# Which queue issues the output stores: double tiles from POOL, half tiles from SyncE

## The chip, the cores and the metric

The kernel runs on one core of a Trainium2 chip. The metric is device time in microseconds (us) of that core, from six runs. The profile is of one execution of its own.

The engines are named as in the profile: PE (TensorE, matmuls) and PEld (its weight loads), DVE (VectorE), ACT (ScalarE), POOL (GpSimd), SP (SyncE). A DMA is issued by an engine into a queue and carried out by 16 DMA engines. In this program the DMAs that POOL issues run on the queue q0, which the profile calls software_dynamic, and those that SyncE issues on q1, hardware_dynamic.

## The reference

The input `x` has 8 sequences of 3264 rows of 192 channels, float32. Two steps follow each other:

```python
# 1: causal convolution over 7 rows, one set of softmax taps per head (8 heads of 24 channels)
w = softmax(weight, axis=-1)
a[b, s] = sum over k of w[h, k] * x_padded[b, s + k]
# 2: spectral mix of the first 64 modes, then a channel mix
X = np.fft.rfft(a, axis=1)
Yr = einsum(Xr, w_r) - einsum(Xi, w_i)      # per mode, 192 x 192
Yi = einsum(Xr, w_i) + einsum(Xi, w_r)
y = np.fft.irfft(Y, n=S, axis=1)
u = a + y
out = u + np.maximum(u @ w_ch, 0.0)
```

The output has the shape of `x`, in float32: 8 x 3264 x 192 x 4 bytes = 20.05 MB.

## The kernel before

The eight sequences are worked on as four pairs, `q` from 0 to 3. A sequence's 3264 rows are 25 tiles of 128 rows (`t` from 0 to 24) and a rest of 64 rows, the half tile. `xall` holds all of the sequences in bfloat16, `slot(q, t)` being the place of one tile of both sequences of a pair.

The kernel has three stages. In the first, `x` is loaded by POOL's DMAs (line 149, cast from float32 to bfloat16 on the way), convolved on PE, copied back into `xall` and transformed into the 64 modes. In the second, the mode weights are loaded, again by POOL (line 426), into buffers in `arena` and in a part of `cc`, and mixed. Both queues and the order on each engine are as written in the program: the schedule is manual.

The third stage, from about 107 us on, makes the output. It goes through the list `duos` (line 530). An item is

- two tiles that follow each other in one pair, `((q, t), (q, t + 1))`: the first four pairs, each with two stores of 192 KB (line 578);
- a double tile, the same `t` in two pairs, `((q, t), (q + 1, t))`: 45 of them, each with one store of 384 KB, 512 rows of 768 bytes (line 573);
- one tile of one pair: the last two items, each with a store of 192 KB (line 563);
- `("h",)`, the half tiles of all pairs, item 14, with four stores of 96 KB from 64 partitions each (line 554);
- an integer 1, 2 or 3 (items 2, 8 and 11), which stores nothing: it makes the spectral coefficients `zw` of that pair.

That makes N = 55 items. For each, PE adds up in a PSUM tile `zt` (four of them, `za` and `zb`, in turn): `c_part` (lines 487 and 494), then `m_part` with which = 0 (line 514), then ACT's `relu` in place (line 540), then `m_part` with which = 1. `finish` (from line 542) has DVE add `xall` to it into a buffer of `outs` (lines 546, 560 and 565), and then the store is issued. The loop at line 622 puts `m_part(n, 0)`, `c_part(n + 1)`, `m_part(n - 1, 1)` and `finish(n - 1)` after one another, so that PE works on three items by turns.

`outs` is six buffers of 3,072 bytes per partition, cut out of `arena`, which holds the mode weights before. Item n uses `outs[n % NO]` with NO = 6. DVE's add into a buffer waits until the store that read the buffer before has landed. An engine issues its DMAs in the order of the program: a store that waits for its add holds back what stands behind it on that engine.

`band` (line 78) holds the taps of the convolution as matrices, 2,048 bfloat16 per partition; nothing reads it after the first stage.

Of the kernel before, what the change touches and what calls it, by code (L numbers as in the profile page):

```python
# [12 lines left out]
F32 = mybir.dt.float32  # L13
# [6 lines left out]
def kernel(  # L20
# [9 lines left out]
    nc = tc.nc  # L30
# [22 lines left out]
    def sb(name, shape, dtype, **kw):  # L53
        return pool.tile([P] + shape, dtype, tag=name, name=name, **kw)
# [23 lines left out]
    band = sb("band", [H, 2 * P], BF16)  # L78
# [18 lines left out]
    NO = 6  # L97
    OB = 2 * 2 * 2 * D
    outs = [arena[:, OB * i:OB * (i + 1)].bitcast(F32).rearrange("p (k d) -> p k d", k=2) for i in range(NO)]
    assert NO * OB <= NW * WGB  # L100
    pos = [0]

    def temp(n, dtype):
# [36 lines left out]
    def slot(q, t):  # L140
        return NT * q + t
# [48 lines left out]
    for g in range(4):  # L190
        dst, srcv = band[32 * g:32 * g + 32, :, 32 * g:32 * g + PW], pk3[32 * g:32 * g + 32, :, :]
# [213 lines left out]
    for k, u in enumerate(units):  # L405
# [5 lines left out]
        if k:  # L411
            q, t0, n = units[k - 1]
# [117 lines left out]
    duos = [((q, t), (q, t + 1)) for q in range(2) for t in (0, 2)]  # L530
# [3 lines left out]
    for k, item in ((2, 1), (8, 2), (11, 3), (14, ("h",))):  # L534
        duos.insert(k, item)

    def relu(n):
        duo, zt = items[n]
        w = D * len(duo) if duo[0] != "h" else 2 * D
        nc.scalar.activation(out=zt[:, :, 0:w], in_=zt[:, :, 0:w], func=ACT.Relu)  # L540

    def finish(n):
        duo, zt = items[n]
        o = outs[n % NO]
        if duo[0] == "h":
            nc.vector.tensor_tensor(out=o[:, :, :].rearrange("p k (a d) -> p k a d", a=2),  # L546
                                    in0=zt[:, :, 0:2 * D].rearrange("p k (a d) -> p k a d", a=2),
                                    in1=xall[:, NF:NF + NT * (NQ - 1) + 1:NT, 0, :].rearrange(
                                        "p (k a) d -> p k a d", k=2), op=ALU.add)
            for k in range(2):  # L550
                for h, r in enumerate(ROWS):
                    dst = bass.AP(tensor=out.tensor, offset=out.offset + ((4 * k + (h ^ k)) * S + P * NF) * D,
                                  ap=[[D, HALF], [2 * S * D, 2], [1, D]])
                    nc.gpsimd.dma_start(out=dst, in_=o[r, k, :].rearrange("p (a d) -> p a d", a=2))  # L554
            return
        (q0, t0), (q1, t1) = duo[0], duo[-1]
        s = [slot(*u) for u in duo]
        ov = o[:, :, :].rearrange("p k (i d) -> p (k i) d", i=2)
        if len(duo) == 1:
            nc.vector.tensor_tensor(out=ov[:, 0:2, :], in0=zt[:, :, 0:D], in1=xall[:, s[0], :, :], op=ALU.add)  # L560
            dst = bass.AP(tensor=out.tensor, offset=out.offset + (2 * q0 * S + P * t0) * D,
                          ap=[[D, P], [S * D, 2], [1, D]])
            nc.sync.dma_start(out=dst, in_=ov[:, 0:2, :])
            return
        nc.vector.tensor_tensor(out=o[:, :, :].rearrange("p k (i d) -> p i k d", i=2),  # L565
                                in0=zt[:, :, 0:2 * D].rearrange("p i (k d) -> p i k d", k=2),
                                in1=xall[:, s[0]:s[1] + 1:s[1] - s[0], :, :].rearrange("p k i d -> p i k d"),
                                op=ALU.add)
        if t0 == t1:

            dst = bass.AP(tensor=out.tensor, offset=out.offset + (2 * q0 * S + P * t0) * D,
                          ap=[[D, P], [S * D, 4], [1, D]])
            nc.sync.dma_start(out=dst, in_=ov)
        else:
            for i in range(2):
                dst = bass.AP(tensor=out.tensor, offset=out.offset + ((2 * q0 + i) * S + P * t0) * D,
                              ap=[[D, P], [P * D, 2], [1, D]])
                nc.sync.dma_start(out=dst, in_=ov[:, i:4:2, :])

    N = len(duos)  # L580
# [41 lines left out]
    for n in range(N + 1):  # L622
        if is_duo(n):
            m_part(n, 0)
            relu(n)
        if n + 1 < N and n > 0:
            if is_duo(n + 1):
                c_part(n + 1)
            else:
                q, zt = items[n + 1]  # L630
                for c in range(2):
                    zw_part(q, c, zt[:, c, :])
                for act, w in enumerate(QUARTERS):
                    zw_copy(zw[:, q, :, w, :], zt[:, :, 0:2 * D].rearrange("p c (b e) -> p c b e", b=4)[:, :, w, :],
                            act)
        if is_duo(n - 1):
            m_part(n - 1, 1)
            finish(n - 1)
# [30 lines left out]
```

## Time and profile before

| | |
|---|---|
| median of six runs | 180.71 us (179.86 to 181.94) |
| the profiled execution: time | 180.41 us |
| the profiled execution: span of the profile | 178.6 us |
| PE, DVE, ACT, POOL busy, share of the span | 83%, 66%, 57%, 38% |
| queue q0 (POOL): packets, bytes | 36224, 20.08 MB |
| queue q1 (SyncE): packets, bytes | 26624, 19.69 MB |
| stores of 384 KB (SyncE, line 573): number, median from issue to landing | 45, 4.4 us |
| stores of 192 KB (SyncE, lines 563 and 578) | 10, 2.8 us |
| stores of 96 KB (POOL, line 554) | 4, 3.4 us |
| HBM read, written | 39.40 MB, 20.05 MB |

The bytes of a queue are counted as they arrive: of a load that casts from float32 to bfloat16, half of what was read. "Busy" of an engine leaves out waiting; issuing a DMA counts as busy for POOL, and for SyncE nothing does. "Landing" is the moment at which the last of the 16 DMA engines has reported. In the views of stretches, a line has the stretch, its length, busy time and number of instructions of each engine, TensorE's granted clock (1.00 is full speed), the mean share of the 16 DMA engines' time that packets took, and GB/s.

### The profile page before, as it was taken

Reading aid. Unit: us, or ns where it says so; the run is one execution under the profiler, and the core shown is the slowest. Engines: PE = TensorE matmul, PEld = TensorE weight load, DVE = VectorE, ACT = ScalarE, POOL = GpSimd, SP = SyncE. Lnnn points to the kernel's source line nnn. Section 1 sums busy time; section 2 is a strip of 40 time slices with the busy share of each in tenths; the row PEclk is TensorE's granted clock in tenths of the full one; section 3 lists DMA queues with packets and bytes.
Section 4 is the critical chain, followed back from the end, with each engine's and each line's share of the span. In section 5 each row is a group of like instructions: output and inputs, shape, how many; then the busy total and the mean of one; then the engine's idle time right before and its main releaser. Section 6 shows DMA issues by size and latency. Waiting matters only on the chain.

```text
span 178.6 us, 6302 instructions
## 1 busy us (share of the span) xinstructions
PE 147.4 (83%) x2736; PEld 108.7 (61%) x2736; DVE 117.0 (66%) x161; ACT 101.6 (57%) x135; POOL 68.3 (38%) x113
## 2 busy tenths in 40 slices
PE   0047789999999998794977768999999999999940
PEld 0033466666666665663865656966677888888820
DVE  1879564766866584564456472795787888888870
ACT  8175755544554636174464566766566766666630
POOL 7999997768865643442336100000140000000000
PEclk9999999999999999999699999999999999999995
DMA  4999999999999999999999970569779999999995
GB/s 46 161 177 187 190 190 190 192 192 194 188 191 192 204 206 206 206 206 207 206 206 206 206 117 4 168 230 317 258 210 359 365 346 369 334 364 359 298 370 178
DMA packets 62875, 40.17 MB, mean 225 GB/s; under 512 B 28800, under 2 KB 62784, under 8 KB 62848
## 3 DMA queue, kind: packets, MB, share of 16 engines
q0 software_dynamic: 36224, 20.08, 80.9%
q1 hardware_dynamic: 26624, 19.69, 32.8%
q8 instruction: 21, 0.34, 0.9%
q14 instruction: 6, 0.05, 0.1%
HBM read 39.40 MB, written 20.05 MB: 333 GB/s over the span
## 4 chain that ended last, share of the span: by engine, by line
DMA 41%; PE 35%; POOL 14%; issue 4%; DVE 2%; POOLq 0%; DVEq 0%
DMA xall<-in_x_dram 17%; DMA arena<-in_moe_w_i_dram 12%; POOL xall L149 10%; PE za L514 9%; PE zb L514 8%; PE za L494 8%; DMA cc<-in_moe_w_i_dram 7%; PE zb L494 7%; DMA arena<-in_moe_w_r_dram 6%; DVE arena L565 1%; POOL xall L219 1%; POOL arena L426 1%; PE zb L521 1%; DVE arena L560 1%; PE low L437 1%
## 5 line engine op out<-in xcount | busy, mean ns | idle before, releaser
L149 POOL DMA_DIRECT2D xall<-in_x_dram x48 | 38.4, 811 | 7.1 <-DMA xall<-in_x_dram 4.9
L305 PE MATMUL z<-xall,band 64*64 64x192 bf16 (+3 forms) x816 | 27.6, 264 | 14.4 <-DVE band L195 10.7
L325 DVE CAST xall<-z 128x768 bf16<-128x768 f32 (+1 forms) x24 | 24.5, 1021 | 13.9 <-PE z L305 10.4
L305 PEld LDWEIGHTS <-band 64*64 64x64 bf16 x816 | 18.4, 110 | 23.0 <-ACT band L193 11.0
L323 ACT CAST xall<-z 128x768 bf16<-128x768 f32 (+1 forms) x24 | 20.4, 850 | 20.7 <-PE z L305 19.6
L494 PEld LDWEIGHTS <-cc 64*128 64x128 bf16 x600 | 27.2, 94 | 6.2 <-issue 1.5
L565 DVE TENSOR_TENSOR arena<-za,xall 128x768 f32<-128x768 f32 x26 | 24.7, 956 | 5.7 <-PE za L514 1.8
L540 ACT ACTIVATE za<-za 128x768 f32<-128x768 f32 (+1 forms) x27 | 21.0, 783 | 8.6 <-PE za L514 8.5
L565 DVE TENSOR_TENSOR arena<-zb,xall 128x768 f32<-128x768 f32 x23 | 21.9, 957 | 4.7 <-ACT za L540 1.8
L540 ACT ACTIVATE zb<-zb 128x768 f32<-128x768 f32 (+1 forms) x25 | 19.6, 782 | 9.2 <-PE zb L514 8.4
L331 PE MATMUL low<-xall,ftab 128*128 128x384 bf16 x100 | 22.0, 348 | 0.0
L385 PEld LDWEIGHTS <-xall 128*128 128x128 bf16 x300 | 19.5, 107 | 3.4 <-issue 0.9
L514 PE MATMUL za<-mixa,ftab 64*128 64x384 bf16 (+1 forms) x120 | 18.1, 304 | 0.0
L514 PE MATMUL za<-mixa,fsin 64*128 64x384 bf16 (+1 forms) x120 | 18.1, 304 | 0.0
L494 PE MATMUL za<-wc,cc 64*128 64x192 bf16 x318 | 17.9, 243 | 0.0
L360 DVE COPY cc<-r 128x1024 bf16<-128x1024 bf16 (+1 forms) x16 | 10.2, 671 | 11.6 <-PE r L385 6.6
L514 PE MATMUL zb<-mixa,ftab 64*128 64x384 bf16 (+1 forms) x100 | 16.1, 313 | 0.4 <-ACT zb L540 0.4
L514 PE MATMUL zb<-mixa,fsin 64*128 64x384 bf16 (+1 forms) x100 | 16.1, 313 | 0.0
L494 PE MATMUL zb<-wc,cc 64*128 64x192 bf16 x282 | 15.9, 243 | 0.0
L514 PEld LDWEIGHTS <-ftab 64*128 64x128 bf16 x220 | 11.9, 94 | 3.9 <-issue 1.5
L358 ACT COPY cc<-r 128x1024 bf16<-128x1024 bf16 (+1 forms) x9 | 8.9, 989 | 8.8 <-PE r L385 7.7
L554 POOL DMA_DIRECT2D out_dram<-arena x4 | 2.4, 617 | 29.8 <-DVE arena L546 29.8
(109 smaller groups left out, 191.3 us busy)
## 6 DMA issues: line engine op xcount, KB each, us to landing
out_dram<-arena SPq DMA_DIRECT2D x45, 384.0 KB, 4.4
xall<-in_x_dram POOLq DMA_DIRECT2D x24, 192.0 KB, 7.3
xall<-in_x_dram POOLq DMA_DIRECT2D x16, 240.0 KB, 6.9
arena<-in_moe_w_r_dram POOLq DMA_DIRECT2D x12, 288.0 KB, 9.2
arena<-in_moe_w_i_dram POOLq DMA_DIRECT2D x12, 288.0 KB, 10.0
out_dram<-arena SPq DMA_DIRECT2D x10, 192.0 KB, 2.8
xall<-in_x_dram POOLq DMA_DIRECT2D x8, 144.0 KB, 6.9
cc<-in_moe_w_r_dram POOLq DMA_DIRECT2D x4, 288.0 KB, 11.3
```

The costliest lines, as they stand in the source:

```text
L149: nc.gpsimd.dma_start(out=xall[:, s0:s0 + nf, i, :], in_=src)
L305: mm = nc.tensor.matmul(ov[c], band[r, h, c.start + shift + 64 * (r is UP and c is LO): c.start + shift + 64 * (r is UP and c is LO) + 64] ...
L323: nc.scalar.copy(out=dst, in_=srcv)
L325: nc.vector.tensor_copy(out=dst, in_=srcv)
L331: nc.tensor.matmul(xp, ftab[:, t, :], xall[:, slot(q, t), :, :], start=(t == 0), stop=False, skip_group_check=True)
L358: nc.scalar.copy(out=out, in_=in_)
L360: nc.vector.tensor_copy(out=out, in_=in_)
L385: nc.tensor.transpose(tp[:, P * k:P * k + P], src, ident[:])
L494: nc.tensor.matmul(zt[:, i, D * k:D * k + D], cc[r, q, 3 * t + j, :], wc[r, j, :], start=(k == 0 and j == 0), stop=False, skip_group_check ...
L514: nc.tensor.matmul(zt[:, i, D * k:D * (k + w)], tabs[c][r, t, :], zw[r, q:q + w, c, QUARTERS[which], :], start=False, stop=end and k + w = ...
L540: nc.scalar.activation(out=zt[:, :, 0:w], in_=zt[:, :, 0:w], func=ACT.Relu)
L565: nc.vector.tensor_tensor(out=o[:, :, :].rearrange("p k (i d) -> p i k d", i=2), in0=zt[:, :, 0:2 * D].rearrange("p i (k d) -> p i k d", k=2),
```

## The change

The stores of double tiles are issued by POOL, except those of the last four items (n of 51 and more), which SyncE issues as before. The half tiles' four stores are issued by SyncE instead of POOL. The half item gets a buffer of its own, cut out of `band`, and the other items that store take the six buffers of `outs` by turns in the order of their stores: the integer items and the half item no longer count. The stores of the first four pairs and of the last two single tiles stay with SyncE. No arithmetic changes.

```diff
@@ -98,6 +98,8 @@
     outs = [arena[:, OB * i:OB * (i + 1)].bitcast(F32).rearrange("p (k d) -> p k d", k=2) for i in range(NO)]
     assert NO * OB <= NW * WGB
+
+    outs.append(band[:, :, :].rearrange("p h c -> p (h c)")[:, 0:OB].bitcast(F32).rearrange("p (k d) -> p k d", k=2))
@@ -534,6 +536,11 @@
     for k, item in ((2, 1), (8, 2), (11, 3), (14, ("h",))):
         duos.insert(k, item)
 
+    buffers = []
+    for duo in duos:
+        buffers.append(NO if duo == ("h",) else sum(b < NO for b in buffers if b is not None) % NO
+                       if isinstance(duo, tuple) else None)
+
@@ -541,7 +548,7 @@
     def finish(n):
         duo, zt = items[n]
-        o = outs[n % NO]
+        o = outs[buffers[n]]
         if duo[0] == "h":
@@ -551,7 +558,7 @@
-                    nc.gpsimd.dma_start(out=dst, in_=o[r, k, :].rearrange("p (a d) -> p a d", a=2))
+                    nc.sync.dma_start(out=dst, in_=o[r, k, :].rearrange("p (a d) -> p a d", a=2))
@@ -570,7 +577,7 @@
-            nc.sync.dma_start(out=dst, in_=ov)
+            (nc.gpsimd if n < N - 4 else nc.sync).dma_start(out=dst, in_=ov)
```

## The prediction

> **What bounds the kernel now.** I read the time first, then the chain of waits, then the stretches of the last stage, then the stores' landings, and last the DMA rate at the very end. The profiled execution took 180.41 us: its span of 178.6 us and 1.8 us around it. It lies 0.3 us under the median of 180.71 us.
>
> Everything that the change touches lies after 113 us. The chain of waits there is TensorE (lines 494 and 514), one piece after another, until 169.2 us; then it is DVE's last adds. The stretches agree (their columns stand in the first line):
>
> ```profile
> core 0: us, PE busy (x) PEld busy (x) DVE busy (x) ACT busy (x) POOL busy (x), PEclk, DMA share, GB/s
> ...
> 140.00:150.00 10.00, 10.00 (x178) 8.25 (x175) 8.32 (x10) 6.94 (x9) 0.00 (x0) 1.00 1.07 359
> 150.00:160.00 10.00, 10.00 (x180) 8.32 (x176) 8.45 (x9) 7.11 (x9) 0.00 (x0) 1.00 1.06 353
> ```
>
> TensorE is never idle, at full clock; DVE, ACT and POOL have room. The DVE adds of line 565 start at 140.66, 141.81, 142.95, 144.10 in the timeline: one item each 1.145 us. An item's 393,216 bytes at the 371 GB/s that the DMA shows when it is full take 1.06 us. So TensorE sets the pace and the stores run 7% below it, a thin margin. The DMA share above 1 says only that packets overlap.
>
> The stores' landings show what the thin margin costs. The last line of each answer is issue to landing; the lines are those of 578 (192 KB, the first pairs), 573 (384 KB) and 563 (the last two, 192 KB):
>
> ```profile
> DMA to landing us min/median/max: 2.0/2.4/4.2
> ...
> DMA to landing us min/median/max: 2.5/4.4/4.9
> ...
> L563 SPq DMA_DIRECT2D out_dram<-arena x2: 558/685/812, 172.6 to 173.2; - x2
> ...
> DMA to landing us min/median/max: 4.5/4.6/4.6
> ```
>
> A 192 KB store with nothing before it lands in 2.0 us; the kernel's very last one needs 4.5. It is issued at 173.25 us, 0.1 after DVE's last add ends (172.58 + 0.56), lands at 177.7, and the program closes 0.9 later. So 2.5 us of the end is queue: the stores before it. What it consists of is in the DMA view of the last 2.6 us (40 bins of 0.065 us):
>
> ```profile
> DMA  9984222211111000000000000000000000000000
> GB/s 378 366 260 130 71 71 71 71 47 47 47 47 36 24 24 24 24 24 24 24 24 0 0 0 0 0 0 0 0 0 0 0 0 0 0 0 0 0 0 0
> ```
>
> All 16 engines write until 176.2 us; then three, two and one of them (a sixteenth of 371 GB/s is 23) until 177.4. A landing needs all 16, so a late engine makes the end late. Why some are late: the queue q8 fetches instructions in packets of 16 KB, 21 in the span, 0.9% of 16 engines' time, so 0.009 x 178.6 x 16 / 21 = 1.2 us each on one engine. With 1.145 - 1.06 = 0.085 us spare per item such a lag needs 14 items to go, and there is a new one every six or so. Around the last one the whole queue also ran dry, though stores were waiting (164.6 to 169 us, 0.11 us a bin):
>
> ```profile
> DMA  9999999999999999996999999999743332222699
> GB/s 377 370 370 363 384 370 356 384 356 349 391 505 342 349 349 342 363 328 203 328 363 335 349 356 335 349 377 321 217 140 112 91 98 77 91 91 91 223 363 370
> ```
>
> For 0.9 us near 168 only about four engines' worth moved; I read it as SyncE's queue not letting the others run on past a late engine. That lost time is still in the queue at the end.
>
> **The change part by part.**
>
> *Who stays.* The first four pairs (t0 unlike t1, eight stores) stay with SyncE; 45 items are double tiles of one t, the last two of them and both single tiles have n of 51 and more and stay too. So 43 stores of 384 KB move to POOL, and the half item's four stores of 96 KB go from POOL to SyncE.
>
> *POOL's time.* POOL does nothing after 99 us but these four half stores, so 43 issues of its own replace idle time.
>
> ```profile
> L149 POOL DMA_DIRECT2D xall<-in_x_dram x48: 740/778/1035, 1.3 to 52.7; - x48
> ...
> L554 POOL DMA_DIRECT2D out_dram<-arena x4: 602/614/638, 129.0 to 130.9; - x4
> ...
> DMA to landing us min/median/max: 2.8/3.4/4.1
> ```
>
> The nearest row is the x load of 512 rows (0.78 us); the ends are 0.60 (128 rows, a store) and 1.04 (the slowest load). All are below 1.145 us, so POOL keeps up: 43 x 0.78 = 34 us of work beside TensorE, cost nothing. If it were over 1.145, each 0.1 us more would be 4.3 us on the end. Before a store POOL also takes 0.29 us to start after DVE (line 546's add ends at 128.73, line 554 starts at 129.02), where SyncE takes 0.03. That delays landings, not the pace. What POOL now waits for is each add; behind its wait is only the next store.
>
> The Trainium skill, "SBUF — State Buffer", section "Who interferes with whom", speaks against POOL here: a DVE instruction in a 2-port mode locks GpSimd out and starves the descriptors. The row beside it: line 554's four issues took 0.60 to 0.64 us while line 565's adds (0.96 us) ran, so this add doesn't lock. By the rule, if it did, a store would cost up to 0.96 + 0.78 = 1.74 us and the end some 25 us.
>
> *Landing of a POOL store and the buffers.* A buffer comes back after six adds: 6 x 1.145 - 0.96 - 0.29 = 5.6 us from POOL's issue. Bounds for the landing: 2.8 (a half store) and 9.0 (an x load, seven outstanding). A load issued on the idle queue needs 4.2, with cast. Built up: 1.15 us from issue to first byte (129.02 to about 130.15 in the DMA view), 0.95 to 1.06 of data, 0.4 to land: 2.6, and up to 1.2 more behind a late engine. I take 3 to 4 us: no wait. DVE's one wait for a store (0.6 us, for the half item's on POOL) goes with the buffer in `band`; it cost TensorE nothing, so it brings nothing. The new count of buffers skips the integer items: a little more room, nothing on the path.
>
> The Trainium skill, "DMA: Bandwidth & Descriptors", section "Issuing engine by pattern", gives a simple store to Sync and calls HWDGE generally faster; its latency table has about 1 us against 0.6 to the first byte. By that each store lands 0.4 us later, within the 5.6, and the sum stays.
>
> *Rate of the software queue.* This is the term that decides. Weights through it arrive at 206 GB/s as bf16, which are 412 GB/s of f32 read; x loads at 190, so 380 read. The store through SyncE never goes over 375 for long. The half stores went out in 192 packets for 0.39 MB, 2 KB each, against 0.75 KB on q1. So a double tile should need 0.95 us (at 412); bounds: 1.03 (at 380), and far above, the half stores beside SyncE's traffic: 58.0% of 16 engines over 1.5 us for 0.19 MB, 29 us per 384 KB or 1.8 us per engine, much of it waiting for the other queue. I take 0.95, as the weights too have long rows and a full queue. Spare time per item becomes 0.19 us: a lag of 1.2 us goes in six items, and with the next store's descriptors already written the queue should not run dry.
>
> *The end.* TensorE and DVE end as now, so the last store is issued at 173.25. Item 50 on POOL: its add ends at 170.25, + 0.29 + 1.15: first byte at 171.7. Then 0.95 for it, 2 x 1.06 and 2 x 0.53 for SyncE's four: 175.8; + 0.3 to land: 176.1, against 177.7. Of the last late engine 1.2 - 3 x 0.19 = 0.6 may be left: 176.7. So 1.0 to 1.6 us less; I take 1.2. POOL's closing drain (6.3 us from 130.4 in the profile, 5.2 after its last issue) would end by 171.3 + 5.2 = 176.5, beside the landing.
>
> Sum: 180.41 - 1.2 = 179.2 for such an execution, 179.5 beside the median.
>
> **The rivals.** About 0.5% (0.9 us) is what a measurement of this kernel can tell from no change.
>
> *The DMA's write rate is the limit, not the queue* (same): 365 to 375 GB/s in every full stretch may be what the memory takes. Then item 50 needs 1.06, lags go as slowly as now, POOL's later start eats what is won: 180.2 to 181.0. For it: how flat the rate is. Against it: the dry 0.9 us, and 412 read. 25%.
>
> *Late buffers* (slower): POOL's stores land later than 5.6 us after issue, and DVE waits for its buffer in each round. At the 7.1 us of the x loads a round of six takes 7.1 + 0.29 + 0.96 = 8.35 us, 1.39 an item: 43 x 0.25 = 10.6 more, 191 us. It starts at 5.6. Against it: those loads queue seven deep. The same place with a smaller excess, 0.1 us an item, gives 185; at 1.8 us of data per item it would be 209. 20% in all, most of it below 186.
>
> *The double tiles don't move*: excluded by the count, if POOL shows 43 issues of 384 KB.
>
> **How the numbers follow.** Forecast 55%, 178.4 to 179.8 with its own bounds (gains of 0.9 to 2.3, the whole queue at most); no change 25%; slower 20%. Faster by over 0.5% is below 179.8, slower above 181.6. For eight in ten the range runs from 178.4 to 181.8: the first two cases and the edge of the third.
>
> **What would show it.** POOL issues of line 580 near 0.78 us, landing in 3 to 4; no DVE wait on a store; adds still each 1.145 us and TensorE's end where it was; the last 192 KB store landing in 3 to 3.5 us instead of 4.5; no dry stretch while stores are queued. I am wrong if adds wait for DMA, if POOL's issues pass 1.1 us, or if the last landing still takes 4.5.

## The result, and the profile after

The changed kernel is slower by a little: 180.95 us (median of 35 runs, 180.18 to 183.02) against 180.17 us for the kernel before (72 runs by now; the first six had 180.71). The ratio is 1.0046, 95% interval 1.0032 to 1.0061, that is 0.8 us (0.6 to 1.1). A second measurement, after2 below, gave 1.0041 (1.0018 to 1.0063). The forecast was 1.2 us faster.

The stores moved as the change says. On the page of the changed kernel, queue lines (packets, MB, share of 16 engines) and POOL's group (busy, mean ns, idle before):

```profile
q0 software_dynamic: 40848, 36.60, 104.4%
q1 hardware_dynamic: 4496, 3.18, 5.6%
...
L580 POOL DMA_DIRECT2D out_dram<-arena x43 | 32.4, 754 | 39.6 <-DVE arena L572 39.0
```

43 stores on POOL, 0.75 us each, far below the 1.145 us of an item. The stores need fewer packets: 26,624 on q1 have become 4,496, and q0 has 4,624 more. TensorE's pace is the same, with POOL now busy beside it:

```profile
core 0: us, PE busy (x) PEld busy (x) DVE busy (x) ACT busy (x) POOL busy (x), PEclk, DMA share, GB/s
140.00:150.00 10.00, 10.00 (x180) 8.38 (x178) 8.31 (x10) 6.85 (x10) 6.73 (x10) 1.00 0.96 359
150.00:160.00 10.00, 10.00 (x178) 8.25 (x174) 8.32 (x10) 6.85 (x10) 6.47 (x10) 1.00 0.92 357
```

The DMA share fell from 1.07 and 1.06 to 0.96 and 0.92 for about the same bytes: the software queue is the quicker one, as forecast. But the landings (line 580 on POOL, then the last two stores on SyncE, line 570) did not become short:

```profile
DMA to landing us min/median/max: 2.9/4.3/5.6
...
L570 SPq DMA_DIRECT2D out_dram<-arena x2: 1027/1138/1248, 172.2 to 173.5; - x2
...
DMA to landing us min/median/max: 3.6/4.0/4.4
```

The last stage can be cut into three terms, each read from the timeline and the landings: from DVE's first add to the end of its last, from there to the last landing, and from there to the end of the span. Each kernel has three profiles, the later ones from runs told of below:

| | adds, us | to the last landing, us | to the end, us | sum, us |
|---|---|---|---|---|
| before | 61.05, 60.97, 61.13 | 4.59, 4.59, 4.61 | 0.90, 0.92, 0.92 | 66.55, 66.47, 66.65 |
| changed | 60.97, 61.56, 61.08 | 4.41, 4.41, 4.41 | 1.33, 1.33, 1.35 | 66.72, 67.31, 66.84 |
| difference of the means | +0.15 | -0.19 | +0.42 | +0.40 |

The +0.15 comes from one profile, the second one of the changed kernel (61.56); its other two, 60.97 and 61.08, are like the kernel before.

What lies before the first add differs by more than that from profile to profile (its start is at 111.5 to 113.6 us in three profiles of the one kernel before), so whole spans of single profiles are not compared.

### The profile page after: what moved, and what is told of

Same layout as the page of the kernel before. It is cut to its first block, busy times and chain, and to the rows that moved or that the text cites. A ratio compares the mean times of both kernels' runs of the same rounds, so it can differ in the third digit from the quotient of the medians.

```text
span 178.4 us, 6296 instructions
## 1 busy us (share of the span) xinstructions
PE 148.6 (83%) x2736; PEld 109.9 (62%) x2736; DVE 116.7 (65%) x161; ACT 101.7 (57%) x135; POOL 98.2 (55%) x152
## 3 DMA queue, kind: packets, MB, share of 16 engines
q1 hardware_dynamic: 4496, 3.18, 5.6%
## 4 chain that ended last, share of the span: by engine, by line
DMA 38%; PE 35%; POOL 18%; issue 4%; DVE 2%; POOLq 0%; DVEq 0%
DMA arena<-in_moe_w_i_dram 18%; DMA xall<-in_x_dram 13%; POOL xall L151 13%; PE za L516 9%; PE zb L516 8%; PE za L496 8%; PE zb L496 7%; DMA cc<-in_moe_w_i_dram 7%; POOL arena L428 1%; DVE arena L572 1%; POOL xall L221 1%; PE zb L523 1%; DVE arena L567 1%; PE low L439 1%; PE zb L508 1%
## 5 line engine op out<-in xcount | busy, mean ns | idle before, releaser
L580 POOL DMA_DIRECT2D out_dram<-arena x43 | 32.4, 754 | 39.6 <-DVE arena L572 39.0
L307 PE MATMUL z<-xall,band 64*64 64x192 bf16 (+3 forms) x816 | 28.3, 268 | 14.5 <-ACT band L195 10.5
L307 PEld LDWEIGHTS <-band 64*64 64x64 bf16 x816 | 18.9, 112 | 23.1 <-ACT band L195 10.9
L333 PE MATMUL low<-xall,ftab 128*128 128x384 bf16 x100 | 22.7, 356 | 0.0
L387 PEld LDWEIGHTS <-xall 128*128 128x128 bf16 x300 | 19.0, 105 | 3.4 <-issue 0.7
L428 POOL DMA_DIRECT2D arena<-in_moe_w_r_dram x12 | 7.4, 615 | 16.3 <-PE low L439 11.9
```

The source lines that it names most:

```text
L307: mm = nc.tensor.matmul(ov[c], band[r, h, c.start + shift + 64 * (r is UP and c is LO): c.start + shift + 64 * (r is UP and c is LO) + 64] ...
L333: nc.tensor.matmul(xp, ftab[:, t, :], xall[:, slot(q, t), :, :], start=(t == 0), stop=False, skip_group_check=True)
L387: nc.tensor.transpose(tp[:, P * k:P * k + P], src, ident[:])
L580: (nc.gpsimd if n < N - 4 else nc.sync).dma_start(out=dst, in_=ov)
```

## The experiments

**The closing checks.** At the end SyncE waits for the completion semaphores of the DMAs, one check after another. This is SyncE's view of its waits, kernel before, then changed kernel: us in total, times, longest.

```profile
SPq L664 <- DMA out_dram<-arena: 3.2, 5, 1.0
```

```profile
SPq L671 <- DMA out_dram<-arena: 2.5, 1, 2.5
```

Before, five checks wait in turn as the stores land, and the last check passes with the last landing: 177.74, closing drain at 177.82. After, one early check waits 2.5 us, until the very last store has landed at 177.09; the seven other checks behind it, already fulfilled, still take 0.06 us each, and the closing drain stands at 177.60. SyncE's DMAs take eight semaphores by turns: the kernel before issues 56 of them there, the changed one 17, so its last store comes round to the semaphore that is checked first.

Two kernels change just that count. a_lane is the changed kernel with 16:

```diff
-                    nc.sync.dma_start(out=dst, in_=o[r, k, :].rearrange("p (a d) -> p a d", a=2))
+                    (nc.gpsimd if (k, h) == (0, 0) else nc.sync).dma_start(out=dst, in_=o[r, k, :].rearrange("p (a d) -> p a d", a=2))
```

> The changed kernel, but with one of the four half stores issued by POOL again, so that SyncE issues 16 DMAs in all instead of 17. Theory 1 (closing checks): DMAs of SyncE take eight completion semaphores by turns, and SyncE checks them at the end in a fixed order, 0.06 us each. In the changed kernel the very last store has the semaphore checked first, so eight checks follow its landing (177.09 landed, 177.605 closing drain: 0.5 us); with 16 DMAs it has the one checked last, so the closing drain follows the landing within 0.1 us and the time is 0.4 to 0.5 us below the changed kernel's, about 180.4 to 180.6 when the kernel before has 180.2. Theory 2 (the later landing alone makes it slower): the order of checks costs nothing that matters, the time stays at that of the changed kernel, 0.7 to 0.8 us above before.

Measured: ratio to before 1.0004 (0.9977 to 1.0031); 0.91 us from the last landing to the end; its waits:

```profile
SPq L671 <- DMA out_dram<-arena: 1.9, 3, 1.0
```

b_lane is the kernel before with 57:

```diff
-                    nc.gpsimd.dma_start(out=dst, in_=o[r, k, :].rearrange("p (a d) -> p a d", a=2))
+                    (nc.sync if (k, h) == (1, 1) else nc.gpsimd).dma_start(out=dst, in_=o[r, k, :].rearrange("p (a d) -> p a d", a=2))
```

> The kernel before, but with one of the four half stores issued by SyncE, so that SyncE issues 57 DMAs instead of 56. Theory 1 (closing checks): the last store's semaphore is now the one checked first, eight checks of 0.06 us follow its landing, and the kernel is 0.4 to 0.5 us slower than before (ratio 1.002 to 1.003) without any store moved to POOL. Theory 2: no difference beyond 0.1 us (ratio 1.000).

```profile
SPq L664 <- DMA out_dram<-arena: 3.5, 1, 3.5
```

The closing is 1.33 us, as expected, but the time is not 0.4 to 0.5 us longer: 0.9986 (0.9958 to 1.0014). So the expectation held for the closing and missed for the time. Its adds take 60.72 us instead of 61.05: the add that waited for the half stores on POOL (0.59, 0.62 and 0.78 us in the three profiles of before) waits no longer. By the profile the two cancel, 66.56 against 66.55.

To have the difference on one chip, the changed kernel and a_lane were run again together.

> The changed kernel itself, once more beside a_lane2 on one chip. What the profiles show of its end is +0.25 us (last landing 0.18 earlier, closing 0.43 longer), the measured ratio 1.0046 is 0.8 us. Theory 1: most of it is the end, the rest is chance: ratio 1.001 to 1.004, and 0.4 us above a_lane2. Theory 3 (something before the last stage is slower too): ratio again 1.004 to 1.006, and a_lane2, which has the same instructions up to there, is only 0.4 below it, so itself at 1.002 or more.

> The kernel a_lane (changed kernel, one half store on POOL, 16 DMAs on SyncE) once more. Theory 1: ratio 0.999 to 1.001, 0.3 to 0.5 us below after2; closing 0.9 us in the profile.

after2 1.0041 (1.0018 to 1.0063), a_lane2 1.0002 (0.9978 to 1.0026): 0.7 us apart, and by the profiles' sums 66.96 against 66.30 (two of a_lane), 0.66. The closing is 0.42 of it. In the profile of after2 the last add waits too. DVE's timeline at the end:

```profile
171.23 0.96 DVE L572 TENSOR_TENSOR arena<-za,xall 128x768 f32<-128x768 f32 x1
172.15 0.56 DVE L567 TENSOR_TENSOR arena<-za,xall 128x384 f32<-128x384 f32 x1
173.14 0.56 DVE L567 TENSOR_TENSOR arena<-zb,xall 128x384 f32<-128x384 f32 x1 [0.43 <-DMA out_dram<-arena]
```

The last add waits for the store of item 48 in the same buffer, which landed at 173.02. The last five adds follow each other in 0.6 to 1 us, so that there the buffer has to come back within 4.4 us of POOL's issue, not 5.6; the store took 4.68. In the first profile DVE has no idle time there, in the third 0.09 us.

These 0.43 us are not a cost of their own. In all three profiles of the changed kernel the last add starts 0.12 us after that landing (172.00 and 172.12, 173.02 and 173.14, 172.29 and 172.41), and the last store of all lands 5.09 us after it, with the stores between landing one behind the other. A longer queue at the end thus moves the wait and the last landing alike.

**The halves of the change.** half_only moves the half tiles' stores and keeps all double tiles on SyncE; double_only moves the double tiles and keeps the half stores on POOL.

```diff
half_only:
-            (nc.gpsimd if n < N - 4 else nc.sync).dma_start(out=dst, in_=ov)
+            nc.sync.dma_start(out=dst, in_=ov)
double_only:
-                    nc.sync.dma_start(out=dst, in_=o[r, k, :].rearrange("p (a d) -> p a d", a=2))
+                    nc.gpsimd.dma_start(out=dst, in_=o[r, k, :].rearrange("p (a d) -> p a d", a=2))
```

> Half of the change: the half tiles' stores on SyncE from their own buffer and the new count of buffers, but all double tiles stay on SyncE. SyncE issues 60 DMAs, so four checks follow the last landing. Theory 1: 0.25 us above before from the checks, nothing else (ratio 1.001 to 1.002). Theory 2 (the move of the doubles is what costs): equal to before (ratio 1.000). If the half stores on SyncE cost of themselves, it is over 0.5 us slower.

> The other half of the change: double tiles on POOL, the half tiles' stores on POOL as before, from their own buffer. SyncE issues 13 DMAs, so three checks (0.2 us) follow the last landing. Theory 1 (closing checks are 0.45 of the 0.8 us): 0.3 us below the changed kernel, about 0.5 above before (ratio 1.003). Theory 2 (POOL's stores land later): as the changed kernel, ratio 1.004 to 1.005. The landing of the last store from the end of the last add tells it: in the changed kernel 4.41 us, before 4.60.

half_only 1.0012 (0.9984 to 1.0040), double_only 1.0023 (0.9992 to 1.0054): the times alone don't tell them apart. The closings do what the counts of 60 and 13 say, 1.15 and 1.10 us; the last landing comes 4.24 and 4.41 us after the last add. So the end has about the same length, 4.2 to 4.6 us, whoever issues. half_only keeps all double tiles on SyncE and still ends earlier after its last add than the changed kernel, so it is not shown that the 0.2 us gained there come from the double tiles on POOL (one profile of half_only and of double_only).

**Is it a queue?** Two kernels leave out the stores of items 45 to 48, those rows of the output not being written, so that the DMA engines catch up before the last six.

```diff
-            nc.sync.dma_start(out=dst, in_=ov)
+            if not 45 <= n <= 48:
+                nc.sync.dma_start(out=dst, in_=ov)
```

> The kernel before without the stores of items 45 to 48 (those rows are not written). Theory A (queue left at the end): item 50 lands 2.5 us after issue, not 4.3, and the last landing comes 2.9 us after the last add, not 4.60: with an empty queue SyncE's path is the shorter one by 0.5 us. Theory B (no queue, the landing itself is slow): 4.5 as before.

> The changed kernel without the stores of items 45 to 48 (those rows of the output are not written), so that the DMA engines have 4.6 us to catch up before items 49 and 50. Read from the end of DVE's last add to the last landing (changed kernel 4.41 us, before 4.60). Theory A (a late DMA engine and its queue are still there at the end): item 50 on POOL lands about 2.9 us after its issue, as the store at 125.97 us did (2.87), not 3.86, and the last landing comes about 3.4 us after the last add. Theory B (a POOL store needs 3.9 us of itself at this place): item 50 still lands 3.8 to 4.0 after its issue and the last landing stays at 4.3 to 4.5.

Kernel before with the gap: the two double tiles after it, then the last two stores.

```profile
L574 SPq DMA_DIRECT2D out_dram<-arena x2: 372/372/373, 169.4 to 170.6; - x2
...
DMA to landing us min/median/max: 2.5/2.5/2.5
...
L563 SPq DMA_DIRECT2D out_dram<-arena x2: 462/490/518, 172.9 to 173.5; - x2
...
DMA to landing us min/median/max: 2.7/2.8/2.8
```

The last landing is 2.89 us after the last add: 1.7 us of the end were queue. The changed kernel with the gap, POOL's timeline and the landings of its two stores:

```profile
163.71 0.75 POOL L581 DMA_DIRECT2D out_dram<-arena  x1 [0.39 <-DVE arena L572]
170.10 1.50 POOL L581 DMA_DIRECT2D out_dram<-arena  x2 [5.64 <-DVE arena L572]
```

```profile
DMA to landing us min/median/max: 2.9/3.2/3.5
```

The first lands 2.9 us after its issue, as expected of an empty queue. But the issue itself is late: the add ended at 169.14, POOL started at 170.10, 0.96 us later instead of 0.30, and the next one starts 0.56 us after its add. The last landing is 4.26 us after the last add, not 3.4 as expected; the late start is at least part of the difference, but no run takes it away alone. So this run shows what a POOL store needs without a queue, and not how much of the changed kernel's end was queue.

The delay goes by a count more than by a place: the 38th double tile on POOL starts 0.96 to 0.99 us after its add in every kernel that has so many, whatever item that is. It is not the only one: the 14th (the 13th in double_only and all_pool) starts 1.36 to 1.43 us after its add. In the changed kernel these are the stores at 137.98 (the DVE add ended at 136.62) and 165.06 (164.10):

```profile
137.98 3.12 POOL L580 DMA_DIRECT2D out_dram<-arena  x4 [1.46 <-DVE arena L572]
...
163.25 0.75 POOL L580 DMA_DIRECT2D out_dram<-arena  x1 [0.39 <-DVE arena L572]
165.06 2.38 POOL L580 DMA_DIRECT2D out_dram<-arena  x3 [1.06 <-DVE arena L572]
```

The engines run dry just after the second one (163.8 to 168.2 us, 0.11 us a bin, the zero at 166.2):

```profile
GB/s 279 433 335 503 377 419 419 349 321 126 210 335 433 461 484 377 391 419 377 140 98 42 0 335 251 517 377 419 419 293 503 209 182 98 573 251 503 377 419 461
```

No row says what POOL waited for; that stays open. Nor is it shown that the late 38th store lengthens the end of the changed kernel. A 16 KB packet of the instruction queue q8 lies in the same stretch (at 165.44, 1.29 us); the landing that comes late is that of the store before the late one (168.08, 2.0 us after the landing ahead of it), and the late store lands 0.98 us behind it, as in a full queue. n11 below has no 38th store on POOL, and its end is no shorter.

**Where POOL should stop.** n3 puts one more double tile on POOL (16 DMAs on SyncE), n11 seven fewer (24 on SyncE, and no 38th on POOL), all_pool everything but the first pairs and two half stores.

```diff
-            (nc.gpsimd if n < N - 4 else nc.sync).dma_start(out=dst, in_=ov)
+            (nc.gpsimd if n < N - 3 else nc.sync).dma_start(out=dst, in_=ov)    # n3; N - 11 in n11
```

> The changed kernel with n < N - 3 in place of n < N - 4: one more double tile on POOL, and SyncE issues 16 DMAs, so that the last landing is on the semaphore that is checked last. Theory 1 (closing checks): from last landing to the end 0.9 us, not 1.33, and the time 0.3 to 0.5 us below the changed kernel's: ratio to before 1.000 to 1.002. Otherwise 1.004 to 1.005. Last landing 4.4 us after the last add in either case.

> The changed kernel with n < N - 11 in place of n < N - 4: the last nine double tiles on SyncE, 36 on POOL, and SyncE issues 24 DMAs (the last landing on the semaphore checked last). POOL's 38th store of a double tile, which started 0.96 us instead of 0.27 after its add in every kernel so far, is gone. Theory A (the end is the queue that is left, and POOL's path is 0.7 us longer): POOL drains the queue to about 1 us, SyncE takes over with its shorter path, and the queue grows again only by the last instruction fetch: last landing 3.6 to 4.2 us after the last add (changed kernel 4.41), closing 0.9 us, ratio 0.997 to 0.999. Theory B (the late DMA engine alone sets the end, whoever issues): last landing 4.3 to 4.6, ratio 0.999 to 1.001.

> The changed kernel with all double tiles and both single tiles on POOL, and two of the half stores too, so that only one or two checks follow the last landing. Theory A (the end is the DMA engines' queue): the last four items move at the software queue's 0.99 us a double tile instead of 1.05, 0.15 us less, but the last one starts 0.27 + 0.4 us later than on SyncE; last landing 4.3 to 4.7 us after the last add, and the time is that of before within 0.3 us, as the closing checks (0.43) are gone. Theory B (POOL's path is slow of itself, SyncE's tail saves it): last landing over 5 us after the last add, ratio over 1.003. A rival of its own: POOL's closing drain ends later than the landing and adds up to 1.5 us.

n3: 0.9994 (0.9961 to 1.0028), closing 0.91, last landing 4.32: the change without its closing cost. n11: 1.0016 (0.9991 to 1.0041), last landing 4.60, closing 0.90: theory B, once SyncE takes over the landings are those of the kernel before. all_pool: 1.0021 (0.9987 to 1.0054), last landing 4.31 us after the last add at 177.24; but POOL's closing drain (of the three, the longest, 4.79 us from 173.2) ends only at 178.0:

```profile
L671 POOLq DRAIN  x3: 46/106/4788, 173.2 to 178.5; - x3
```

so the closing is 1.54 us. POOL's drain does become the last thing when POOL issues to the end.

**Both repairs.** Two more profiles of before and one of the changed kernel are in the table above; best is a_lane with the last single tile in the half item's buffer.

> The kernel before, a second profile. From DVE's first add of the last stage to the end: 66.55 us in the first profile. If the wait of one add for the half stores on POOL (0.59 us, at 135.13) belongs to the kernel, it is there again with 0.3 to 0.6 us, and the stage from first to last add is again 61.0 to 61.3; if it was chance, there is no such wait and the stage is 60.7.

> The kernel before, a third profile, for the same question; last landing 4.5 to 4.6 us after the last add, closing 0.90.

> The changed kernel, a third profile. If the last single tile's add waits for its buffer as a rule (the store of item 48, six adds before), it shows 0.1 to 0.5 us of DVE waiting for a store after 171 us; if after2 was chance, none. Closing 1.33 us, last landing 4.4 after the last add.

```diff
+    buffers[-1] = NO
```

> a_lane (changed kernel, one half store on POOL, 16 DMAs on SyncE) with the last single tile in the half item's buffer, so that its add waits for no store. If closing checks and late last buffer are all that makes the changed kernel slower: ratio 0.997 to 1.000, no add waits for a store after 171 us, closing 0.9. If something else is in it, 1.001 or more.

best: no add waits at the end, closing 0.92, sum of the stage 66.38, and still 1.0020 (1.0000 to 1.0040). The buffer of its own brings nothing beside a_lane, whose sums are 66.21 and 66.39: the wait goes, the last landing stays. None of these kernels is shown to be faster than the one before. The sums of the stage put a_lane, n3, half_only and best 0.2 to 0.3 us below before; the measured times put them between 0.1 us below and 0.4 us above. This rest, 0.1 to 0.5 us from kernel to kernel, and with it about 0.4 of the 0.8 us of the changed kernel, is not located: no term of the stage shows it, and before the stage the profiles scatter by more.

## Why the prediction was wrong

**POOL's time and TensorE's pace: right.** 0.75 us a store for 0.78, 43 of them, nothing on the path. The section of the Trainium skill that the prediction weighed ("SBUF — State Buffer", "Who interferes with whom") does not speak against POOL here, as the prediction has it: it says that `tensor_tensor` has no 2-port mode, and this add, a TENSOR_TENSOR, takes one of its inputs from PSUM. The trace agrees: POOL's issues took 0.75 to 0.81 us beside every add.

**The rate: right in kind.** Landings that follow each other with a queue behind them are 0.98 to 1.00 us apart on POOL (155.24, 156.24, 157.23, 158.22), 1.04 to 1.12 on SyncE before; I had 0.95 and 1.06. The rival of a flat write rate has the measured time in its range (180.2 to 181.0). Its rate is wrong, since POOL's landings are not 1.06 us apart; its other half, that POOL's later start eats what is won, is what happened.

**The end: the term that failed.** It was to give 1.0 to 1.6 us and gave 0.2. The step that failed is the landing of item 50: 2.7 us after the end of its add in my sum, 3.3 with a late engine; measured, 4.16 (4.31 in the kernel before). It was to land at 172.9, or 173.6 with a late engine; in the changed kernel the adds came 0.43 to 0.46 us earlier, so at 172.5 to 173.1, and it landed at 173.98. The last line of each answer, first for the store at 126 us with no queue before it, kernel before and changed kernel, then for item 50 in the changed kernel (4.28 before):

```profile
DMA to landing us min/median/max: 2.5/2.5/2.5
```

```profile
DMA to landing us min/median/max: 2.9/2.9/2.9
```

```profile
DMA to landing us min/median/max: 3.9/3.9/3.9
```

Two parts of my sum were too small. The first is the path. A POOL store with no queue before it needs 3.16 us from the add's end to the landing, 0.30 until it starts and 2.87 from there (the one at 125.97; 2.92 from the start in after_gap), and I had built up 2.7; SyncE's needs 2.49, 0.03 and 2.46. (The Trainium skill's "HWDGE generally faster", in "DMA: Bandwidth & Descriptors", "Issuing engine by pattern", holds here for this path, by 0.7 us, and not for the rate.)

The second is the queue. I let it be empty but for 0.6 us of one late engine, after counting three items of catching up at 0.19 us. The changed kernel's landings show the true sum: 4.0, 3.8, then 4.6 after an instruction packet, 4.4, and down 0.15 an item again. At 0.15 us an item and a packet about every six items, what one packet adds is about what is caught up (from 151 us on: 0.75 up and 0.62 down, 0.87 up and 0.97 down), and from 137 us on the queue never goes below 1.0 us (3.8 against 2.87). That the packets cause the jumps is read from the times alone; no run leaves one out. The kernel before has 1.7 (4.13 against 2.46), as before_gap shows, too. So POOL's queue is 0.7 us shorter, and POOL's path is 0.7 longer: the gain was given back on the path of each store.

SyncE's last four stores then took 3.11 us, for which I had 3.18. The very last one took 3.57 us from its issue, near the 3 to 3.5 that was to be a sign of success. The sign misled: SyncE issued it 0.84 us after its add (0.11 before), and from the add's end it landed only 0.2 us sooner. The dry stretch, which was to go, has stayed.

**The closing: not in the sum.** I carried 0.9 us from the last landing to the end over as if fixed. It depends on which check the last landing answers, and became 1.33. The count of DMAs on SyncE was in my own text; what follows from it at the end I did not ask.

**The wait for the half stores: right by luck.** I said that it cost TensorE nothing, so that the buffer in `band` brings nothing. The wait does cost: from the add of item 17 to that of item 22 the three profiles of before take 5.94, 5.97 and 6.13 us, b_lane without the wait 5.72, and the changed kernel 5.73. But from item 13 to item 17 the changed kernel takes 4.99 instead of 4.81 (before and b_lane), because the add behind the half item comes later. DVE's line in before, then in the changed kernel:

```profile
129.01 0.96 DVE L565 TENSOR_TENSOR arena<-zb,xall 128x768 f32<-128x768 f32 x1 [0.28 <-ACT za L540]
```

```profile
128.98 0.96 DVE L572 TENSOR_TENSOR arena<-zb,xall 128x768 f32<-128x768 f32 x1 [0.64 <-PE za L516]
```

Why is open; half_only has the same 4.99. Taken together, items 13 to 22 need 10.72 us instead of 10.75 to 10.94: next to nothing, but not for my reason.

**Late buffers: the rival was there, but small.** Not in every round, as it was priced (10.6 us). In the first profile of the changed kernel one add waits for a store that took 5.64 us, just over the 5.6 of my sum:

```profile
140.38 0.96 DVE L572 TENSOR_TENSOR arena<-za,xall 128x768 f32<-128x768 f32 x1 [0.33 <-DMA out_dram<-arena]
```

The adds have made that up by 142.53. The other is the last add, where items are shorter and the 5.6 us do not hold: 0.43 us in one profile of three, as told above no cost of its own.

## What to carry to other kernels

A queue's rate helps only what is left after its path: compare the landing of a lone store on either queue, from the end of the producing instruction, before crediting a faster rate with a shorter end. Look at what follows the last landing: which check it answers cost 0.4 us here, twice what the end had gained. And a buffer's return time is to be taken where the items are shortest, not at the steady pace: there a buffer came back late first, though here the wait cost nothing of its own.

## What the runs showed of the hardware that I had not expected

- A check of a fulfilled semaphore on SyncE takes 0.06 us at the end, and eight of them behind the last landing instead of one cost 0.43 us (closings of 0.90, 1.10, 1.15 and 1.33 us in kernels with 56, 13, 60 and 57 or 17 DMAs on SyncE).
- A POOL store starts 0.30 us after its add as a rule, but the 38th double tile on POOL 0.96 us after it, also in the kernel where another item stood there, and the 14th (in two kernels the 13th) 1.36 to 1.43 us. The cause is open.
- POOL's closing drain ended 0.6 us after the last landing of a POOL store in the changed kernel (174.57 after 173.98) and 0.75 after it in all_pool, where it set the end. That is no fixed time: in the kernel before, whose last POOL store is a half store, it was 1.65 us.
